# A list of steps in a new order: loads, lead-in, key rows, operand sums, x transposes and stores of an attention-and-MLP kernel

## The chip, the cores and the metric

The kernel runs on one core of a Trainium2 chip. Time is device microseconds of one execution; the number compared is the median of several runs. A core has five instruction streams that run side by side: TensorE (PE, matrix products; the loading of its weights is shown apart as PEld), VectorE (DVE), ScalarE (ACT), GpSimd (POOL) and SyncE (SP). Each works through its instructions in order and stops at one whose semaphores have not come yet. Transfers are issued by one of these streams (here POOL and SP) and carried out by 16 DMA engines.

## The reference

The inputs are q, k and v of shape 4 x 8 x 768 x 64 (batch, heads, tokens, head size), w_in 512 x 2048 and w_out 2048 x 512, all float32. Cut to what is computed:

```python
k_sum = k.reshape(B, H, 24, 32, D).max(axis=3)      # one key per block of 32 tokens
v_sum = v.reshape(B, H, 24, 32, D).mean(axis=3)
scores_l = where(|i - j| < 16, q @ k.T / 8, -1e9)    # local window
scores_s = q @ k_sum.T / 8 + log(32)                 # 24 block summaries
a = softmax(concatenate([scores_l, scores_s], -1))
x = a @ concatenate([v, v_sum])                      # then heads side by side: 3072 x 512
h = x @ w_in
out = (h * sigmoid(1.702 * h)) @ w_out               # 3072 x 512
```

## The kernel before

The work is cut by batch (768 tokens, four batches) and a batch into two halves of 384 tokens. Every step has a name, and the whole program is one list of 1001 such words, ORDER (line 35 on). The loop at the end of the kernel calls the step for each word in turn. A wrapper (line 28, the line that the profile gives for nearly every instruction) keeps the instructions of each engine in the order in which they were called. A word is a name and arguments separated by dots: numbers are the batch, half, head pair or tile and often the PSUM bank, and a last letter a, d or g puts a copy or sum on ACT, DVE or POOL. So the list sets, for each engine and each queue of transfers, what stands behind what; how far engines run apart is left to the semaphores.

The steps that the change and the prediction name:

- Loads, all issued by POOL: Lk, Lq, Lv (keys, queries, values of batch 0), Li (w_in in five pieces, two of 256 KB and three of 512 KB in float16), Lo (w_out in four), and lk, lq, lv for the later batches, one head or one strip each. Eight semaphores serve these loads, so a load waits until the eighth before it has landed. gate.1 and gate.2 are tiny POOL copies that hold the loads behind them back until a value strip or an x transpose is there.
- Lead-in of batch 0: T and Q turn keys and queries on PE, To and Qc copy them out, km takes key maxima of blocks; sm, so, sx, em, ed, ex, bt, bx make the scores and exponentials of the first half, vt and vc the block sums of v, ao, ab, ae the weighted values, vn the division by the row sum, xt and xc the transpose of x. lo, lh, lr, vo, vr, cv, ck, ow lay out keys and values for the common path; mk and mf are the masks.
- Common path: s are scores of a half and head pair, e their exponentials, m the mask, v the weighted values, nn the division, t and c (batches 0 and 1) or d (batches 2 and 3, a DMA transpose on SP) the transpose of x. Keys and queries are turned on PE for batch 1 (tk, kc, tq, qc, xm, kh, kr) and by DMA transposes on SP for batches 2 and 3 (xk, xq, then xa, ka, kR for block maxima, halos and rows). ha, sd, vm and vb make the halo and block-sum rows of the values; ha and sd are DMAs on SP.
- First product f (x by w_in, 128 columns of w_in by 384 tokens, four matmuls each, into PSUM tile ph), then g, the activation into gT.
- Second product p.t.w: the product with w_out for two strips of 128 tokens by a seven-product scheme. It reads gT, operand sums of gT (gs, the last number is the kind: product 5 reads kind 0, 6 kind 1, 7 kind 2, 3 kind 3), w_out and operand sums of w_out (ws: product 5 reads 0, 6 reads 1, 7 reads 2, 4 reads 3). x takes a product out of PSUM, o stores a strip on SP.
- P7.0 closes the pool "even", which holds the buffers of batches 0 and 2 (kx0, qT0, vw0); with the argument 0 nothing is opened in its place.

The stages follow one another, with attention of the next batch laid between the second products of this one: lead-in, first products of batch 0, its second products with scores and values of batch 1, first products of batch 1, and so on to the second products of batch 3.

```python
    for word in ORDER.split():
        name, *args = word.split(".")
        ops[name](*[engines[a] if a in engines else ...])
```

Of the kernel before, what the change touches and what calls it, by code (L numbers as in the profile page):

```python
# [45 lines left out]
lk.1.2 lv.1.5.1 lk.1.5 lk.1.6 lq.1.2 lk.1.7 m.1.1 lq.1.1 lv.1.0.0 lq.1.4 lq.1.5 lq.1.7 lv.1.3.1 lq.1.6 lv.1.0.1
lv.1.2.0 lv.1.1.0 cv.1 lv.1.1.1 lv.1.4.0 lv.1.2.1 f.0.8.k0123.2 lv.1.4.1 late m.1.3 ws.0.0 g.0.8 f.0.9.k0123.3
f.0.11.k0123.0 g.0.9 f.0.10.k0123.1 v.0.1.0.40 v.0.1.1.41 lv.1.3.0 nn.1.0 g.0.11 lv.1.5.0 g.0.10 v.0.1.2.50 v.0.1.3.51
nn.1.1 f.0.12.k0123.2 g.0.12 f.0.13.k0123.3 g.0.13 t.1.0.42 c.1.0.d f.0.14.k0123.1 g.0.14 f.0.15.k0123.0 t.1.1.52
c.1.1.d f.1.0.k01.2 f.1.8.k01.3 f.1.1.k0123.1 ws.1.0 g.0.15 g.1.1 f.1.0.k23 ws.2.0 f.1.8.k23 g.1.0 g.1.8 ws.0.1 ws.1.1  # L50
# [10 lines left out]
lv.2.1.0 lq.2.1 lv.2.0.1 lq.2.4 lv.2.3.1 lv.2.4.0 lq.2.6 m.1.0 lv.2.4.1 p.1.6 lq.2.5 p.1.2.0 x.1.6.a s.1.0.2.52
s.1.0.3.42 e.0.2 p.2.1.2 e.0.3 p.1.7 x.1.7.a s.1.1.2.52 e.1.2 s.1.1.3.42 e.1.3 x.1.2.a m.0.2 x.2.1.a p.1.3 x.1.3.a
lq.2.7 o.0.1.0.0.2 v.1.0.0.50 m.1.3 v.1.0.1.51 p.1.4 x.1.4.a o.0.1.1.0.2 p.2.5.1 x.2.5.a m.0.3 v.1.1.0.40 v.1.1.1.41
nn.0.0 p.2.6 x.2.6.a nn.1.0 t.0.0.52 m.1.2 c.0.0.a p.2.2.3 x.2.2.a t.1.0.42 c.1.0.a p.2.7 x.2.7.a v.1.0.2.50
v.1.0.3.51 nn.0.1 v.1.1.2.40 v.1.1.3.41 p.2.3 x.2.3.a o.0.2.0.0.2 p.2.4 t.0.1.52 f.0.1.k01.0 nn.1.1 x.2.4.a
o.0.2.1.0.2 f.0.8.k01.1 f.0.9.k01.3 c.0.1.d f.0.0.k01.2 G f.0.0.k23 t.1.1.42 c.1.1.d f.0.8.k23 f.0.9.k23 f.0.1.k23
g.0.0 g.0.8 g.0.1 g.0.9 xk.0.0.0 xk.0.0.1 xk.0.1.0 xk.0.1.1 xq.0.0 xq.0.1 f.1.0.k0123.2 f.1.8.k0123.1 g.1.0
f.1.1.k0123.0 g.1.8 g.1.1 f.1.9.k0123.3 g.1.9 gs.0.2.0 gs.0.2.1.g gs.0.2.3 f.0.2.k0123.2 g.0.2 f.0.10.k0123.0
f.1.2.k0123.1 xa.0.0 g.1.2 gs.0.2.2.d g.0.10 f.1.10.k0123.3 g.1.10 f.0.3.k0123.2 g.0.3 f.1.3.k0123.1 g.1.3 gs.2.2.2.d
f.1.11.k0123.3 g.1.11 ha.2.2.0 xa.1.0 gs.2.2.0 f.0.11.k0123.0 g.0.11 gs.2.2.1 gs.2.2.3 f.0.4.k0123.2 g.0.4  # L70
# [894 lines left out]
```

## Time and profile before

| | us |
|---|---|
| median of 3 runs | 211.71 |
| the runs | 211.71, 211.21, 211.89 |
| span of the profiled execution | 211.4 |
| PE busy | 198.6 (94%) |
| DVE, ACT, POOL busy | 128.1, 117.4, 109.1 |
| lead-in, to the steady first products | 26.3 |
| second products of batch 0 begin | 51.1 |
| first products of batches 1, 2, 3 begin (on both halves) | 77.3, 125.3, 168.5 |
| last matmul ends | 207.7 |

The page gives the profiled execution no time of its own beside its span; its span lies 0.3 us under the median. The profile has one row for a group of instructions: engine, operation, what it writes and reads, count and duration. A wait row has the engine, what waited, what it waited for, and total, times and longest. The chain follows the work that ended last back to the start: PE holds 71% of it, transfers 15%. The granted clock is full (1.00) in every stage up to the last.

### The profile page before, as it was taken

Reading aid. Unit: us, or ns where it says so; the run is one execution under the profiler, and the core shown is the slowest. Engines: PE = TensorE matmul, PEld = TensorE weight load, DVE = VectorE, ACT = ScalarE, POOL = GpSimd, SP = SyncE. Lnnn points to the kernel's source line nnn. Section 1 sums busy time; section 2 is a strip of 40 time slices with the busy share of each in tenths; the row PEclk is TensorE's granted clock in tenths of the full one; section 3 lists DMA queues with packets and bytes.
Section 4 is the critical chain, followed back from the end, with each engine's and each line's share of the span. In section 5 each row is a group of like instructions: output and inputs, shape, how many; then the busy total and the mean of one; then the engine's idle time right before and its main releaser. Section 6 shows DMA issues by size and latency. Waiting matters only on the chain.

```text
span 211.4 us, 5837 instructions
## 1 busy us (share of the span) xinstructions
PE 198.6 (94%) x2416; PEld 143.2 (68%) x2416; DVE 128.1 (61%) x311; ACT 117.4 (56%) x227; POOL 109.1 (52%) x157
## 2 busy tenths in 40 slices
...
GB/s 73 159 166 192 206 224 212 179 136 123 98 155 191 161 166 180 132 149 126 151 159 202 166 161 169 196 169 87 3 99 68 188 99 0 0 3 0 99 102 99
DMA packets 96458, 27.74 MB, mean 131 GB/s; under 512 B 85024, under 2 KB 93488, under 8 KB 96432
## 3 DMA queue, kind: packets, MB, share of 16 engines
...
HBM read 27.26 MB, written 6.29 MB: 159 GB/s over the span
## 4 chain that ended last, share of the span: by engine, by line
PE 71%; DMA 15%; POOL 9%; issue 2%; DVE 2%; POOLq 0%
PE ph L28 31%; PE poA L28 19%; PE poB L28 9%; DMA w_out_sb<-in_moe_w_out_dram 7%; DMA kb<-in_k_dram 4%; PE poC L28 4%; DMA xT<-x 4%; PE ps_s L28 3%; PE ps_av L28 2%; POOL v0n L28 2%; POOL w_in_sb L28 2%; POOL kx L28 2%; PE ps_t L28 1%; POOL kb L28 1%; POOL qb L28 1%
## 5 line engine op out<-in xcount | busy, mean ns | idle before, releaser
L28 PE MATMUL ph<-xT,w_in_sb 128*128 128x384 f16 x512 | 86.0, 326 | 0.7 <-DMA xT<-x 0.7
L28 ACT ACTIVATE gT<-ph 128x384 f16<-128x384 f32 x128 | 58.7, 495 | 23.8 <-PE ph L28 22.9
L28 PEld LDWEIGHTS <-w_in_sb 128*128 128x128 f16 x512 | 49.2, 98 | 32.3 <-issue 0.9
L28 PEld LDWEIGHTS <-gs 128*128 128x128 f16 x384 | 36.3, 98 | 4.7
L28 PEld LDWEIGHTS <-gT 128*128 128x128 f16 x288 | 27.5, 98 | 3.7
L28 DVE TENSOR_TENSOR gs<-gT 128x768 f16<-128x768 f16 (+1 forms) x36 | 17.1, 490 | 21.1 <-ACT gT L28 21.0
L28 ACT ACTIVATE a_sb<-ps_s 128x768 bf16<-128x768 f32 x32 | 24.5, 808 | 9.0 <-PE ps_s L28 8.9
...
L28 PE MATMUL poA<-ws,gs 128*128 128x256 f16 x192 | 24.9, 273 | 0.0
L28 POOL TENSOR_TENSOR gs<-gT 128x768 f16<-128x768 f16 x4 | 6.9, 1727 | 33.9 <-ACT gT L28 33.9
L28 ACT ACTIVATE s<-poA 128x256 f32<-128x256 f32 x14 | 5.4, 384 | 20.3 <-PE poA L28 19.0
L28 DVE TENSOR_TENSOR a_sb<-a_sb,mk 128x768 bf16<-128x768 bf16 x28 | 14.6, 549 | 3.0 <-POOL mk L28 1.9
L28 DVE TENSOR_TENSOR x<-ps_av,rc 128x768 f16<-128x768 f32 (+1 forms) x18 | 15.6, 868 | 0.6
L28 POOL TENSOR_TENSOR gs<-gs,gT 128x768 f16<-128x768 f16 (+1 forms) x6 | 8.4, 1404 | 13.0 <-DVE gs L28 12.9
L28 DVE TENSOR_TENSOR gs<-gT,gs 128x768 f16<-128x768 f16 (+1 forms) x19 | 9.2, 489 | 6.1 <-POOL gs L28 5.5
L28 PE MATMUL poB<-ws,gs 128*128 128x256 f16 x96 | 12.5, 273 | 0.0
L28 PE MATMUL poB<-w_out_sb,gs 128*128 128x256 f16 x96 | 12.5, 273 | 0.0
L28 PE MATMUL poA<-ws,gT 128*128 128x256 f16 x96 | 12.5, 273 | 0.0
L28 PE MATMUL poC<-w_out_sb,gT 128*128 128x256 f16 x96 | 12.4, 273 | 0.0
L28 PE MATMUL poA<-w_out_sb,gT 128*128 128x256 f16 x96 | 12.3, 273 | 0.0
...
## 6 DMA issues: line engine op xcount, KB each, us to landing
out_dram<-osb SPq DMA_DIRECT2D x23, 256.0 KB, 3.5
kb<-in_k_dram POOLq DMA_DIRECT2D x24, 96.0 KB, 6.0
qb<-in_q_dram POOLq DMA_DIRECT2D x24, 96.0 KB, 5.5
...
kb<-in_k_dram POOLq DMA_DIRECT2D x4, 192.0 KB, 4.2
```

The lines of the kernel that those rows point to most:

```text
L28: r = f(*a, **kw)
```

## The change

Only ORDER changes: the same 1001 steps stand in another order, with other PSUM banks, and some copies and sums on another engine. In words:

- Loads of batch 0: the first query load goes ahead of the keys, all of batch 0 ahead of w_in; the loads of batch 1 begin ahead of the last piece of w_in, and three of the four quarters of w_out are strewn among them (Lo.1, then Lo.3, Lo.0 and Lo.2; Lo.2 is the 38th load). The value loads of batch 2 and gate.1 move.
- Lead-in: the edges of the values (cv), vo and the rows of keys come earlier, vr near the end; all scores of batch 0 come ahead of the first f. To, Qc, vc, xc and lo change engines.
- Operand sums: five of the eight ws move behind the first second product of batch 0; gs are dealt anew, with 20 on POOL in the list instead of 11.
- Key rows: kR.0 and ka.0 of batch 2 come before vb and the sums of gT, ka.0 on DVE; kh and kr of batch 1 change engines.
- x transposes: d.1.1 and d.1.0 of batch 2 change places. P7.0 moves from the end of the list into the first products of batch 2. In the built program, xk.1.0.1 and xk.1.0.0 (batch 3) stand ahead of d.1.1 and d.1.0 in SP's queue, although the list has them behind.
- Stores and the copies x move within the second products; the last ones stay last.

The diff, cut to the parts spoken of:

```diff
 ORDER = """
-start Lk.0 X Lk.1 id Lq.0.0 Lk.2 Lk.3 Lq.0.1 Lv.0 Lv.1 Lv.2 cs I.10.512 sel on T.0.2 Li.1 Lv.3 To.0.a ba I.2.128 km.0
-sm.0.42 Li.0 sm.1.52 T.1.1 To.1.a Lq.1.0 Lq.1.1 I.3.128 Q.0.0.0 Qc.0.0.a Qc.0.1.d so.0 sx.0 km.1 T.2.1 To.2.a so.1
-sx.1 T.3.0 em.2 ed.0 ex.0.1 ex.0.0 bt.0.1 bx.0 To.3.d Q.0.1.0 Qc.0.2.d sm.2.42 so.2 sx.2 Qc.0.3.d sm.3.52 Li.4 so.3
-sx.3 km.2 vt.0.2.1 vc.0.2.d km.3 ao.0.40 ao.1.41 ab.0 ab.1 ae.1 ae.0 vn.0 vn.1 ed.1 ex.1.0 bt.1.0 ex.1.1 lh.3.g bx.1
-vt.2.1.1 vc.2.1.d ao.2.2 xt.0.3 lh.0.d ab.2 xc.0.d lh.1.g ae.2 vn.2 vt.3.1.1 vc.3.1.a ao.3.1 ck.0 xt.1.3 lo.0.g lh.2.g
-xc.1.a ab.3 lo.1.g ae.3 vn.3 cvs vr Li.2 lr.0.g lr.1.g Q.1.0.42 Qc.1.0.a Qc.1.1.a s.0.1.0.52 e.1.0 Li.3 Lo.0 vo.0.d
-xt.2.0 xt.3.1 vo.1.d mk.0 Lo.2 mk.1 Lo.1 Lo.3 xc.2.a xc.3.a f.0.0.k01.2 Q.1.1.0 Qc.1.2.a s.0.1.1.42 e.1.1 ow.0 cv.0
-sd.0.0.3 ha.0.2.3 sd.0.1.3 ha.0.3.3 ha.0.0.3 lk.1.0 f.0.0.k23 ha.0.1.3 Qc.1.3.d s.0.1.2.52 f.0.1.k01.3 e.1.2
+Lq.0.0 cvs Lk.0 start id on I.10.512 Lk.1 Lk.2 ba I.2.128 Q.0.0.1 ow.1 T.0.2 I.3.128 T.1.0 cs To.0.d Lq.0.1 Qc.0.1.a X
+Lk.3 Qc.0.0.a Lv.1 ck.0 To.1.a sm.0.42 Lv.0 T.2.0 Lv.2 sm.2.52 sel Q.0.1.1 mk.0 so.0 To.2.d Lv.3 Lq.1.0 em.0 km.0
+Qc.0.2.a T.3.2 ow.0 sx.0 Lq.1.1 To.3.d Li.2 so.2 km.1 sm.1.42 lh.3.g ed.0 Qc.0.3.a km.2 km.3 sx.2 cv.1 so.1 sm.3.52
+cv.0 vt.0.2.1 ex.0.1 sx.1 so.3 ex.0.0 vc.0.2.a ed.1 bt.0.2 lr.0.g bx.0 ex.1.0 ao.0.40 vt.2.1.2 sx.3 ex.1.1 ao.1.41
+ab.1 lo.1.g lo.0.d ab.0 bt.1.3 ao.2.1 vo.1.d ae.0 lh.0.d vc.2.1.a ae.1 lr.1.g lh.1.g Q.1.0.52 vt.3.1.0 Li.0 bx.1
+ao.3.2 vn.0 Qc.1.0.a lh.2.g Qc.1.1.a s.0.1.0.52 vo.0.d e.1.0 ab.2 Li.1 vn.1 ae.2 Q.1.1.3 vc.3.1.a vn.2 Li.3 s.0.1.1.42
+ab.3 ha.0.2.3 Qc.1.3.d Qc.1.2.a e.1.1 ae.3 mk.1 xt.1.0 xt.2.1 xt.0.3 s.0.1.3.42 xc.1.a xc.2.a vn.3 xc.0.d s.0.1.2.52
+e.1.3 xt.3.2 vr e.1.2 mf sd.0.1.3 xc.3.d m.1.2 ha.0.3.3 f.0.0.k01.0 f.0.1.k01.1 sd.0.0.3 f.0.0.k23 f.0.4.k0123.40
+ha.0.0.3 g.0.0 lv.1.2.1 f.0.6.k0123.50 ha.0.1.3 lv.1.1.0 f.0.5.k0123.41 f.0.1.k23 f.0.7.k0123.51 g.0.6 g.0.4 ck.1
+f.0.8.k0123.0 Li.4 Lo.1 g.0.1 g.0.8 f.0.10.k0123.2 late g.0.7 m.1.3 f.0.9.k0123.1 f.0.11.k0123.0 lk.1.0 g.0.5 lv.1.5.0
...
-f.1.3.k0123.2 g.1.3 f.1.11.k0123.1 g.1.11 gs.2.2.0 gs.2.2.1 gs.2.2.2 f.1.12.k0123.3 gs.2.2.3 g.1.12 f.1.4.k0123.2
-tk.0.52 kc.0.a f.1.13.k0123.0 g.1.13 ws.3.1 g.1.4 f.1.5.k0123.1 g.1.5 tk.1.52 gs.4.2.2 kc.1.a f.1.14.k0123.3 tk.2.42
-kc.2.a f.1.6.k0123.2 g.1.6 gs.4.2.0 gs.4.2.1 gs.4.2.3 gs.6.1.2 g.1.14 gs.6.1.0 gs.6.1.1 gs.6.1.3 f.1.7.k0123.1 g.1.7
-f.1.15.k0123.0 g.1.15 gs.7.1.0 tk.3.52 tq.0.42 kc.3.d gs.7.1.1 gs.7.1.2 p.0.1.2 x.0.1.a kh.1.1.d xm.0.1 kr.0.1.d
-ha.1.3.0 kh.0.1.d p.1.1.3 qc.0.a p.0.5.1 x.0.5.a ha.1.2.0 tq.1.52 qc.1.a p.0.6 x.0.6.a tq.2.42 gs.7.1.3 qc.2.a xm.1.1
+g.0.12 Lo.3 c.1.1.d lv.1.3.1 lv.1.5.1 f.1.6.k0123.3 f.1.3.k0123.1 g.1.6 f.1.14.k0123.2 g.1.14 lk.1.2 f.1.2.k0123.0
+g.1.3 tk.0.52 ws.0.1 f.1.0.k01.2 f.1.9.k0123.1 g.1.2 lq.1.1 kc.0.a f.1.0.k23 lk.1.5 lk.1.3 gs.6.1.0 xm.0.1
+f.1.11.k0123.0 g.1.9 kr.0.1.d f.1.7.k0123.3 G f.1.15.k0123.1 Lo.0 g.1.11 g.1.0 f.1.1.k0123.0 lv.1.0.0 g.1.7 lk.1.6
+ws.2.1 g.1.15 g.1.1 gs.6.1.1 lv.1.2.0 lk.1.7 f.0.15.k0123.2 ws.1.1 gs.7.1.0 f.1.12.k0123.1 gs.6.1.2 gs.7.1.2
+f.1.8.k01.0 f.1.8.k23 tk.2.52 g.1.12 Lo.2 g.1.8 kc.2.a lq.1.4 lq.1.5 lq.1.2 gs.0.2.2 tq.0.42 lq.1.7 f.1.10.k0123.3
+f.1.4.k0123.1 g.1.10 tk.1.52 kh.0.1.d gs.2.2.2 gs.0.2.0 g.1.4 qc.0.d gs.7.1.1 f.1.13.k0123.3 g.0.15 f.1.5.k0123.0
+xm.2.1 p.0.1.2 g.1.5 gs.2.2.0 s.1.0.0.42 g.1.13 kc.1.d gs.0.2.1 lq.1.6 ws.0.0 gs.4.2.0 p.1.1.3 p.0.5.1 e.0.0 x.0.1.a
+tk.3.52 lq.1.3 gs.4.2.1 lv.1.4.1 x.0.5.a kc.3.a gs.2.2.1 gs.6.1.3 p.0.2.0 ws.1.0 lv.1.1.1 p.0.6 ws.2.0 lv.1.0.1
+x.0.2.a lv.1.3.0 lv.1.4.0 x.0.6.a gs.4.2.3 gs.0.2.3 gs.4.2.2 gs.2.2.3 gs.7.1.3.g tq.2.52 qc.2.a xm.1.1 x.1.1.a p.1.2.0
+p.0.7 ha.1.3.0 kr.1.1.d p.0.3 tq.3.42 lk.2.4 tq.1.52 kh.1.1.g x.0.3.a p.1.6 ha.1.2.0 qc.3.d xm.3.1 kr.2.1.d kh.2.1.g
+vm.1.42 vb kr.3.1.g x.0.7.a qc.1.a s.1.0.1.52 kh.3.1.g p.1.5.1 lq.2.4 x.1.6.a e.0.1 ws.3.0 s.1.1.0.52 x.1.5.a lq.2.0
+lq.2.1 s.1.1.1.42 p.1.7 lv.2.0.1 ws.3.1 e.1.1 p.0.4 e.1.0 lk.2.0 lk.2.5 lq.2.3 s.1.0.3.42 s.1.0.2.52 p.1.3 e.0.3
...
-s.1.1.1.52 e.1.1 m.0.1 vm.1.42 vb sd.1.1.0 kr.2.1.g kh.3.1.d sd.1.0.0 xm.3.1 kr.3.1.d p.1.5.1 gate.1 lv.2.3.0 lv.2.1.1
+f.0.3.k0123.1 f.1.2.k0123.0 g.1.9 gate.1 lq.2.6 f.1.0.k0123.3 g.1.2 g.0.3 f.1.11.k0123.2 f.1.13.k0123.1 xk.0.0.0 g.1.0
...
-f.1.4.k0123.1 g.1.4 f.1.12.k0123.3 g.1.12 f.0.12.k0123.0 f.0.5.k0123.2 g.0.12 ka.0.g f.1.5.k0123.1 g.0.5
-f.0.13.k0123.0 g.0.13 f.1.13.k0123.3 g.1.5 f.0.6.k0123.2 vm.2.42 g.1.13 g.0.6 gs.4.2.0 gs.4.2.2.d vb sd.2.0.0
-f.1.6.k0123.1 sd.2.1.0 f.0.14.k0123.0 g.1.6 g.0.14 f.1.14.k0123.3 gs.4.2.1 g.1.14 gs.6.1.0 f.1.7.k0123.2 ha.2.0.0
-g.1.7 f.0.15.k0123.0 ha.2.3.0 g.0.15 gs.6.1.1 f.0.7.k0123.1 g.0.7 kR.0.d f.1.15.k0123.3 g.1.15 gs.7.1.0 X gs.6.1.3
-p.0.1.2 s.2.0.1.52 e.0.1 s.2.0.0.42 lv.3.1.0 lk.3.0 lk.3.4 lv.3.1.1 lk.3.2 gs.7.1.1 lk.3.7 lk.3.3 ha.2.1.0 x.0.1.d
+f.0.15.k0123.1 f.1.5.k0123.2 g.0.15 gs.2.2.2.d xq.0.1 lv.2.4.1 xa.1.0 lk.3.0 vm.2.42 f.0.13.k0123.1 g.1.5
+f.1.15.k0123.2 kR.0.d g.1.10 lv.3.4.1 f.0.7.k0123.0 g.0.13 f.1.14.k0123.3 f.0.4.k0123.1 vb g.0.7 g.1.14 f.0.5.k0123.0
+ka.0.d g.1.15 gs.2.2.0 lv.3.3.1 g.0.4 f.1.7.k0123.3 s.2.0.0.52 lv.3.1.0 g.0.5 s.2.0.1.42 o.0.2.0.0.2 gs.0.2.1.g
+gs.6.1.0 gs.0.2.3 gs.4.2.2.d p.0.1.0 g.1.7 p.0.2.2 e.0.0 gs.4.2.0 p.1.1.3 gs.7.1.0 gs.2.2.1.g sd.2.0.0 sd.2.1.0
+x.0.1.d gs.7.1.1 gs.7.1.2.g o.0.2.1.0.2 lk.3.4 gs.4.2.1 gs.6.1.1.g o.0.1.1.0.2 gs.7.1.3 x.0.2.a m.0.0 e.0.1 gs.2.2.3
...
-x.1.3.a o.1.1.0.0.2 nn.0.1 d.0.1 p.2.1.2 x.2.1.d p.1.4 v.2.1.0.40 v.2.1.1.41 nn.1.0 x.1.4.d v.2.1.2.50 v.2.1.3.51
-nn.1.1 p.2.5.1 x.2.5.a d.1.0 p.2.6 d.1.1 gate.2 lq.3.6 p.2.2.3 x.2.6.a p.2.7 x.2.7.a p.2.3 G x.2.2.a x.2.3.a
-o.1.2.0.0.2 p.2.4 x.2.4.a f.0.1.k01.0 f.0.9.k01.3 f.0.0.k01.2 f.0.0.k23 xk.1.1.0 xk.1.0.1 f.0.8.k01.1 f.0.8.k23
-p.2.4 x.2.4.d P7.0 o.3.1.1.0.2 o.3.2.1.0.1
+x.1.5.a p.1.3 lk.3.7 p.2.5.1 v.2.1.2.50 X lk.3.3 x.1.7.a o.1.0.1.0.2 d.0.0 d.0.1 v.2.1.0.40 lv.3.0.0 x.2.5.a
+v.2.1.1.41 x.1.3.a G v.2.1.3.51 nn.1.1 p.2.1.2 lq.3.1 x.2.1.d lk.3.2 o.1.1.0.0.2 p.1.4 d.1.1 p.2.2.0 nn.1.0 lv.3.2.1
+x.1.4.a lv.3.5.1 p.2.6 p.2.3 x.2.2.a x.2.6.a gate.2 lv.3.3.0 p.2.7 x.2.3.a d.1.0 x.2.7.a f.0.0.k01.1 f.0.9.k01.3 P7.0
+f.0.1.k01.0 xk.1.0.1 f.0.9.k23 lk.3.5 f.0.0.k23 lv.3.4.0 f.0.1.k23 g.0.9 g.0.0 xk.1.0.0 p.2.4 xk.1.1.1 g.0.1
+f.0.4.k0123.1 x.2.4.d f.1.2.k0123.0 g.1.2 f.1.10.k0123.2 f.1.1.k0123.3 lv.3.0.1 g.0.4 f.0.8.k01.0 g.1.10 g.1.1
+"""
```

More of the change, by code (lines that the diff above doesn't have):

```diff
@@ L46 @@
[L46 to L50, printed above, removed]
@@ L61 @@
[L61 to L65, printed above, removed]
@@ L66 @@
[L66 to L70, printed above, removed]
@@ new lines @@
+v.1.1.1.41 lk.2.1 o.0.0.1.0.2 lv.2.0.0 x.2.6.a x.1.7.a x.2.5.a nn.0.0 nn.1.0 p.2.7 p.2.2.0 p.1.4 m.1.2 t.1.0.52
+o.0.1.0.0.2 t.0.0.42 c.1.0.d lk.2.6 p.2.3 c.0.0.a v.1.0.2.50 x.2.7.a lk.2.3 x.2.2.a v.1.0.3.51 lv.2.1.1 x.2.3.a
+v.1.1.2.40 v.1.1.3.41 lk.2.2 lq.2.2 f.0.8.k01.1 p.2.4 nn.0.1 lv.3.1.1 t.0.1.52 x.2.4.d f.0.1.k01.0 x.1.4.a lq.2.5
+c.0.1.d f.0.9.k01.3 f.0.0.k01.2 f.0.9.k23 nn.1.1 f.0.0.k23 f.0.1.k23 f.0.8.k23 G t.1.1.42 xk.0.0.1 g.0.0
+f.0.11.k0123.2 g.0.9 g.0.8 g.0.11 c.1.1.d g.0.1 f.1.8.k0123.1 f.1.1.k0123.3 lv.2.5.0 lq.2.7 g.1.8 g.1.1 f.1.9.k0123.2
@@ new lines @@
+f.0.3.k0123.1 f.1.2.k0123.0 g.1.9 gate.1 lq.2.6 f.1.0.k0123.3 g.1.2 g.0.3 f.1.11.k0123.2 f.1.13.k0123.1 xk.0.0.0 g.1.0
+lv.2.3.0 xa.0.0 g.1.13 xk.0.1.1 f.0.2.k0123.0 lv.2.2.1 lv.2.4.0 g.1.11 f.0.6.k0123.3 f.1.3.k0123.1 g.0.2 xk.0.1.0
+g.0.6 lv.2.5.1 f.0.12.k0123.2 f.0.10.k0123.0 lv.2.2.0 g.1.3 gs.0.2.0 g.0.12 f.1.4.k0123.3 xq.0.0 gs.0.2.2.g
+f.1.6.k0123.2 lv.2.3.1 g.1.4 g.0.10 f.1.12.k0123.1 g.1.12 f.1.10.k0123.0 g.1.6 lv.2.1.0 f.0.14.k0123.3 g.0.14
+f.0.15.k0123.1 f.1.5.k0123.2 g.0.15 gs.2.2.2.d xq.0.1 lv.2.4.1 xa.1.0 lk.3.0 vm.2.42 f.0.13.k0123.1 g.1.5
```

71 lines of the change are left out of this document (34 added, 37 removed).

## The prediction

> **What bounds the kernel now.** I read the page's busy shares and its chain first, then the waits of TensorE (PE), then the stages, and inside a stage the timelines of the engines that PE waits for. The page:
>
> ```profile
> PE 198.6 (94%) x2416; PEld 143.2 (68%) x2416; DVE 128.1 (61%) x311; ACT 117.4 (56%) x227; POOL 109.1 (52%) x157
> PE 71%; DMA 15%; POOL 9%; issue 2%; DVE 2%; POOLq 0%
> ```
>
> PE is the bound: 94% busy of a span of 211.4 us. After the change the list holds the same matmuls, so only PE's idle time and its thin first stage can move. Its idle time by what ended it (total, times, longest):
>
> ```profile
> PE ps_s L28 <- issue: 1.8, 1, 1.8
> PE ps_t L28 <- DMA kb<-in_k_dram: 1.0, 1, 1.0
> PE ph L28 <- DMA xT<-x: 0.7, 1, 0.7
> PE ps_av L28 <- DMA vw<-vw: 0.7, 1, 0.7
> PE ps_s L28 <- DVE kx L28: 0.3, 1, 0.3
> ```
>
> And by stage (start:end, length, then the busy time of PE, PEld, DVE, ACT and POOL, the granted clock, DMA share, GB/s):
>
> ```profile
> 0.00:26.30 26.30, 21.71 (x390) 13.11 (x390) 18.64 (x67) 14.12 (x26) 24.37 (x47) 1.00 1.39 159
> 26.30:51.10 24.80, 23.11 (x218) 14.86 (x211) 18.25 (x39) 18.09 (x38) 16.28 (x27) 1.00 1.68 179
> 51.10:77.30 26.20, 25.91 (x446) 21.73 (x445) 21.65 (x55) 14.84 (x25) 20.93 (x32) 1.00 1.51 149
> 99.60:125.30 25.70, 23.20 (x361) 19.28 (x360) 18.04 (x44) 11.49 (x19) 14.61 (x20) 1.00 2.11 162
> ```
>
> None of these waits lies behind 125.3. So there is something to win before it (some 4 us of waits, and the lead-in up to 26.3), and behind it only something to lose. The clock is 1.00 and drops out. The first wait also shows how to count:
>
> ```profile
> 32.60 0.22 PE L28 MATMUL ps_av<-vw,a_sb 128*64 128x65 bf16 x1
> 33.50 0.67 PE L28 MATMUL ps_av<-vw,a_sb 128*64 128x65 bf16 x31 [0.68 <-DMA vw<-vw]
> ```
>
> From start to start it is 0.90, because a matmul lasts 0.22 but would let the next start almost at once. So each wait costs 0.2 more than its idle row: 0.9, 1.2 (ps_t), 2.0 (ps_s) and 0.9 (ph).
>
> **1. Lead-in.** Before, the steady run of first products begins at 26.32:
>
> ```profile
> 26.32 1.96 PE L28 MATMUL ph<-xT,w_in_sb 128*128 128x384 f16 x11
> qb<-in_q_dram POOLq DMA_DIRECT2D x2, 192.0 KB, 8.8
> w_in_sb<-in_moe_w_in_dram POOLq DMA_DIRECT2D x2, 256.0 KB, 8.1
> 8.00:12.00 4.00, 3.06 (x84) 2.07 (x78) 2.42 (x4) 3.57 (x8) 4.00 (x6) 1.00 1.83 165
> 10.06 0.53 PE L28 MATMUL ps_k<-wide,kb 128*64 128x128 bf16 x12
> L28 DVE TENSOR_REDUCE ks<-qT 128x24 bf16<-128x768 bf16 x4 | 3.8, 946 | 0.9 <-ACT qT L28 0.9
> L28 DVE TENSOR_TENSOR x<-ps_av,rc 128x384 f16<-128x384 f32 x4 | 2.2, 558 | 0.1
> L28 DVE COPY vw<-v0n 64x1536 bf16<-64x1536 bf16 x1 | 0.7, 696 | 0.0
> L28 DVE MEMSET vw<- 32x264 uint32 x4 | 1.1, 278 | 0.4
> L28 DVE COPY vs<-vs 24x128 bf16<-24x128 bf16 x4 | 0.8, 203 | 0.1
> L28 DVE COPY qT<-ps_q 128x384 bf16<-128x384 bf16 x4 | 2.1, 556 | 1.4 <-ACT qT L28 0.8 <-PE ps_q L28 0.6
> ```
>
> By the first row a first-product matmul costs (1.96 - 0.33)/10 = 0.163 us, 0.33 being the last one's own length. Ten are done ahead of 26.32, so the run could as well have begun at 24.7. The last two query loads go out near 12 and land 8.8 later, at 21; the new list takes two 256 KB pieces of w_in from ahead of them, at 165 GB/s 3.2 us, so queries come at 18. The bound is then DVE. The last key load is sixth instead of fifth, so its transposes move from 10.06 to about 11.0 and end at 11.5. Behind them DVE has To.3 0.96, three key maxima 2.84, the edges of the values (cv, moved here from later) 1.40, vo.0 and vo.1 1.39, four normalisations of 0.75 (the 558 row and a reciprocal of 0.19), lo.0 and lh.0 0.9, one Qc 0.56, vr 0.81, two copies of x transposed 0.72. That is 12.6 us: the run starts at 24.1 with four matmuls done, as if at 23.4, so 1.3 earlier. Ends: 0 (DVE idles between them as before, 7.7 of 26.3 us) and -2.3 (queries were the limit). DVE is not quite without gaps, as vn waits for PE each time; I take **-1.0**. The moves of To, Qc and vc between ACT and DVE are in this sum. Masks and constants cost nothing, since POOL makes them before the first mask at 28; one late would cost its 0.3.
>
> **2. First values.** v.0.1 needs the halo and block-sum copies, which SP issues:
>
> ```profile
> 26.48 2.36 SPq L28 DMA_DIRECT2D vw<-vw  x3
> vw<-vw SPq DMA_DIRECT2D x1, 33.0 KB, 5.1
> ```
>
> In the new list vr is next to last on DVE, done at 23.7; SP's copies behind it come 0.6 apart (2.36 for three, with gaps), the last issued at 26.3 and landed 5.1 later, 31.4. PE has 40 matmuls to do first: 23.4 + 6.5 = 30.0. So 1.4 instead of 0.9: **+0.5** (0 to +1.5).
>
> **3. Batch-1 keys and w_out.** Loads on POOL land in order of issue. Those of batch 1 now stand ahead of three quarters of w_out:
>
> ```profile
> 21.09 14.38 DMA w_out_sb<-in_moe_w_out_dram
> 35.76 9.50 DMA kb<-in_k_dram
> ```
>
> This chain, POOL waiting on w_out and tk.0 on keys issued behind it, goes. The first key pair is in with 5.4 MB, by the stages' 159 and 179 GB/s (0.6 MB of SP's counted in) at 36.3; tk.0 comes at 38.9. **-1.2**, at worst 0. The price: w_out's third quarter is now the 38th load. It is in with 8.0 MB and 0.7 of SP's, at 51.5; the operand sum that feeds the second products wants it at 52. That is cover of 0.5 us only; I take **+0.3** (0 to 2.5).
>
> **4. DVE under batch 0's second products.** Of the eight operand sums of w_out (ws, 0.69 each) five move behind the first product: ws.0.0 ahead of gs.4.2.0, which p.0.5 reads, ws.3.1 behind vb. DVE has 21.65 of 26.20 in this stage already. Step by step against the products' 0.87, p.0.5 is 0.3 late, p.0.7 0.5, p.0.4 0.8, while the 0.3 on kx goes with 0.2 behind it: **+1.1** (0 if DVE comes 1.5 early, +3 if every ws counts).
>
> **5. Scores of batch 2.** Before:
>
> ```profile
> 101.33 0.52 DVE L28 COPY kx<-ka 128x576 bf16<-128x576 bf16 x2
> 101.73 0.67 PE ps_s L28 x24
> ```
>
> kR.0 (101.33) sits behind vb and the sums of gT, and the scores behind it: 2.0. The new list puts it ahead of both, and ka.0 on DVE instead of POOL: **-2.0** (at worst 0).
>
> **6. x transposes of batch 2, on SP.** The list itself is harmless here: d.1.1 and d.1.0 stand ahead of xk.1.0.1 and xk.1.0.0. But P7.0, which closes the pool holding kx0, qT0 and vw0, moves from the end into this batch's first products, and the built program's SP queue has those two transposes of batch-3 keys *ahead* of d.1.1 and d.1.0. They wait for the last of four key loads, lk.3.2, and all behind them on SP waits too.
>
> ```profile
> 114.76 1.25 SPq L28 DMA_TRANSPOSE xT<-x  x1
> 117.39 5.70 SPq L28 DMA_TRANSPOSE xT<-x  x3
> 125.67 2.66 SPq L28 DMA_TRANSPOSE kx<-kb  x2
> 123.47 1.14 PE L28 MATMUL ph<-xT,w_in_sb 128*128 128x384 f16 x6
> DMA to landing us min/median/max: 2.8/3.9/7.9
> kb<-in_k_dram POOLq DMA_DIRECT2D x24, 96.0 KB, 6.0
> ```
>
> (The fifth row is xT's.) The products of batch 1 start at 98.3 on the new clock. POOL has three operand sums there until 101.3, then eleven issues of about 0.8 before lk.3.2, at 111; it lands at 117.0. Two xk 2.66: 119.7; d.1.1 1.25: 120.9; d.1.0 lands between 3.9 and 7.9 after that, and I take the middle, 5.9, as loads still run: 126.8. PE began these first products at 123.47; in the new list one product (0.87) moves behind that start, and the first matmul on half 1 has it and 16 first-product matmuls ahead, so 126.1 on the old clock. Parts 1 to 5 and 7's vm make that 2.0 earlier, 124.1, and with the wait for d.0, which stays behind nn.0 and is again about 0.9, it is 125.0. So 1.8 more wait on d.1.0, and with 0.3 for its own start behind two SP stores: **+2.1**. Ends: 0 (lk.3.2 issued by 109) and +5 (7.9, and two us of POOL delay).
>
> [...]
>
> **7. Small ones.** vm.2 waits for lv.2.4.1, issued behind gate.1 and a POOL sum: **+0.3** (0 to 1.4). In batch 3, gate.2 reads the late d.1.1 and holds lk.3.5, behind it xk.1.1, ka.1 and xq.1:
>
> ```profile
> POOL gate L28 <- DMA xT<-x: 8.4, 1, 8.4
> 178.81 1.51 DVE L28 TENSOR_TENSOR gs<-gT 128x768 f16<-128x768 f16 x1 [3.88 <-ACT gT L28]
> 178.27 1.63 POOL L28 TENSOR_TENSOR gs<-gT 128x768 f16<-128x768 f16 x1 [0.25 <-ACT gT L28]
> L28 DVE TENSOR_TENSOR gs<-gT,gs 128x768 f16<-128x768 f16 x12 | 6.6, 556 | 6.0 <-POOL gs L28 5.5
> ```
>
> Before, POOL waited 8.4 there and PE not at all; s.3.0 may now be **+0.5** late (0 to 2.5). POOL's operand sums rise from 11 to 20, and a DVE sum beside one took 1.51 instead of 0.556: **+0.35** (0 to 2). PE changes its kind of matmul 77 times instead of 87, at about 0.1 where it counts: **-0.2**. Copies of products (x), stores and PSUM banks: nothing, as ACT is busy 56% and DVE 61%; without that cover a copy costs its 0.4. The end, a copy and a 128 KB store, stays.
>
> [...]
>
> **Sum.** -1.0 + 0.5 - 1.2 + 0.3 + 1.1 - 2.0 + 2.1 + 0.3 + 0.5 + 0.35 - 0.2 = +0.75, say 0.8. Against the profiled execution that is a span of 212.2. The page gives it no other time; the median of the three runs is 0.3 above its span, so 212.5.
>
> **Rivals.**
> B, faster: SP's order costs nothing and batch 3 is in time. It decides by lk.3.2: issued by 109, d.1.0 is there by 125. For it speaks that POOL issued loads 0.8 apart in the old trace, against it that it waited for sums and landings too. Then 2.1 and 0.5 go: 209.9.
> C, slower: w_out's third quarter. From 52 on each us late holds DVE's queue at ws.1.0 and PE with it; the queue landed w_out 14.4 after issue at worst. 2.5 late gives 2.2 more than my 0.3: 214.7.
> D, slower: POOL's sums meet DVE's. At 0.95 for eight of the nine new ones on PE's path the 0.35 becomes 2.9, if DVE has no slack before the reader: 215.
> E, gains and losses cancel, 211.7, with lead-in at -1.8.
>
> **Chances.** Forecast 212.5, 38%, its own range 212.4 to 214.2; B 30%, C 13%, D 7%, E 12%. The range 209.3 to 215.6 reaches from B with more of the lead-in to the ends of C and D. A measurement here tells some 0.3% from no change: faster 0.30, same 0.12, slower 0.58.
>
> **What will show it.** The steady run of first products from about 24; v.0.1 waiting on vw<-vw 1.4; no wait of ps_t on kb, none of ps_s near 100; ph waiting on xT some 2.5 in sum; on SP kx<-kb ahead of the last two xT<-x. I am wrong if poA or poB waits for w_out or ws, if xT's wait is below 1, or if DVE idles in the lead-in as before.

## The result, and the profile after

The changed kernel takes 220.12 us (median of 4 runs, 217.27 to 220.28); the kernel before took 211.8 beside it (4 runs, 211.21 to 214.69). The ratio is 1.0352, with a 95% interval of 1.0272 to 1.0432. The prediction was 212.5, with a range up to 215.6: the sign was right, the size was not. The profiled execution took 220.11 with a span of 218.4; in the runs that have both, the time is some 1.7 us above the span, so the profiled execution of the kernel before, with its span of 211.4, took about 213.1, above its median. Spans are compared with spans below: 218.4 against 211.4, 7.0 more. The medians lie 8.3 apart, so about 1.3 of the difference is not in this pair of profiles.

First the busy line of the page and PE's waits in the changed kernel (total, times, longest):

```profile
PE 200.5 (92%) x2416; PEld 143.8 (66%) x2416; DVE 138.2 (63%) x299; ACT 112.4 (51%) x225; POOL 122.6 (56%) x171
PE ps_av L28 <- DMA vw<-vs: 2.8, 1, 2.8
...
PE poA L28 <- DVE s L28: 1.7, 3, 1.0
PE ps_s L28 <- DMA qT<-qb: 1.5, 1, 1.5
...
PE ps_av L28 <- DMA vw<-vw: 0.9, 1, 0.9
PE poB L28 <- DVE osb L28: 0.9, 1, 0.9
PE ph L28 <- DMA xT<-x: 0.6, 1, 0.6
```

The waits that the change was forecast to remove are gone: none of ps_t on kb, and none of ps_s near 100. Three others have come: the first values on the copies of value rows (vw), products on DVE (poA, poB), and the scores of batch 3 on their queries. Two numbers of the first line matter for later. PE is busy 2 us longer with the same 2416 matmuls, and DVE 10 us longer (138.2, before 128.1) although it has fewer instructions (299, before 311).

The largest loss is at the first values. The timeline of PE there, and the same stretch by windows (start:end, length, busy time of PE, PEld, DVE, ACT and POOL with their counts; the third number from the end is the granted clock):

```profile
25.11 6.87 PE L28 MATMUL ph<-xT,w_in_sb 128*128 128x384 f16 x40
...
34.78 0.19 PE L28 MATMUL ps_av<-vw,a_sb 128*64 128x65 bf16 x1 [2.80 <-DMA vw<-vs]
35.89 1.28 PE L28 MATMUL ps_av<-vw,a_sb 128*64 128x65 bf16 x47 [0.92 <-DMA vw<-vw]
37.10 3.99 PE L28 MATMUL ph<-xT,w_in_sb 128*128 128x384 f16 x16
```

```profile
26.00:33.00 7.00, 5.94 (x36) 3.25 (x34) 2.23 (x8) 5.76 (x12) 5.91 (x8) 1.00 1.26 167
33.00:36.00 3.00, 0.30 (x8) 0.25 (x10) 0.00 (x0) 0.27 (x1) 0.70 (x1) 1.00 1.42 205
36.00:38.00 2.00, 2.00 (x50) 1.47 (x49) 1.38 (x4) 0.00 (x0) 0.68 (x1) 0.55 2.34 155
38.00:40.00 2.00, 2.00 (x9) 0.99 (x8) 0.91 (x1) 0.66 (x2) 1.82 (x3) 0.60 1.58 189
40.00:42.00 2.00, 2.00 (x22) 1.48 (x21) 0.53 (x2) 1.19 (x3) 2.00 (x3) 1.00 1.75 181
```

The run of 40 first products ends near 32. The first value matmul starts at 34.78, the second at 35.89: 4.1 us lost from start to start, against 0.9 before. Behind this gap the granted clock is 0.55 and 0.60 for four microseconds. Sixteen matmuls take 3.99 there, where the pace of the kernel before makes 15 x 0.163 + 0.33 = 2.8, and the 47 value matmuls 1.28 instead of about 0.93 (48 take 0.95 with the halos first, below); that is 1.6 more. The one run of the four at 217.27 had a mean clock of 0.998, the others 0.984 to 0.992, as if the clock had fallen in those three; the mean does not say where. In this profile, then, 3.9 us almost without a matmul are followed by 0.55 to 0.60 of the clock for about 4 us; going by the mean clocks, that was not so in every run. Less idle time came ahead of a low clock too: the profile of the run with exchanged key loads, below, has 0.50 behind a wait of only 1.0.

Where the 7.0 us came from, start to start, with the terms of the prediction:

| place | before | after | difference | predicted |
|---|---|---|---|---|
| lead-in, first products as if begun at | 24.7 | 25.1 | +0.4 | -1.0 |
| first values: gap, then half clock | 0.9 | 4.1 + 1.6 | +4.8 | +0.5 |
| tk on keys | 1.2 | 0 | -1.2 | -1.2 |
| w_out; DVE in batch 0's products | 0.5 | 0.9 | +0.4 | +0.3, +1.1 |
| batch 2 scores and the products around | 2.0 | 1.5 | -0.5 | -2.0 |
| x transposes of batch 2 | 0.9 | 0.8 | -0.1 | +2.1 |
| batch 3: scores, then products on DVE | 0 | 3.2 | +3.2 | +0.85 |
| last products, on DVE | 0 | 0.6 | +0.6 | 0 |

With the forecast's -0.2 for PE's own order, which no row here measures, that is +7.4, within 0.4 of the 7.0 found. The lead-in row holds for this pair of executions alone (see part 1, below).

### The profile page after: what moved, and what is told of

It reads as the page before. It is cut to its first block, busy times and chain, and to the rows that moved or that the text cites. A ratio compares the mean times of both kernels' runs of the same rounds, so it can differ in the third digit from the quotient of the medians.

```text
span 218.4 us, 5834 instructions
## 1 busy us (share of the span) xinstructions
PE 200.5 (92%) x2416; PEld 143.8 (66%) x2416; DVE 138.2 (63%) x299; ACT 112.4 (51%) x225; POOL 122.6 (56%) x171
## 5 line engine op out<-in xcount | busy, mean ns | idle before, releaser
L28 PE MATMUL ph<-xT,w_in_sb 128*128 128x384 f16 x512 | 87.4, 329 | 0.7 <-DMA xT<-x 0.6
L28 ACT ACTIVATE gT<-ph 128x384 f16<-128x384 f32 x128 | 57.0, 491 | 42.1 <-PE ph L28 41.0
L28 PEld LDWEIGHTS <-w_in_sb 128*128 128x128 f16 x512 | 49.7, 99 | 33.3 <-issue 1.6
L28 DVE TENSOR_TENSOR gs<-gT 128x768 f16<-128x768 f16 (+1 forms) x31 | 20.3, 678 | 23.0 <-ACT gT L28 22.8
L28 POOL TENSOR_TENSOR gs<-gT 128x768 f16<-128x768 f16 (+1 forms) x9 | 14.3, 1595 | 34.0 <-ACT gT L28 34.0
L28 PEld LDWEIGHTS <-gT 128*128 128x128 f16 x288 | 27.8, 98 | 4.0
L28 POOL DMA_DIRECT2D qb<-in_q_dram x28 | 23.3, 844 | 1.6 <-POOLq L949 0.8
L28 DVE TENSOR_TENSOR a_sb<-a_sb,mk 128x768 bf16<-128x768 bf16 x28 | 16.5, 614 | 2.3 <-ACT a_sb L28 2.3
L28 PE MATMUL poB<-w_out_sb,gs 128*128 128x256 f16 x96 | 12.6, 273 | 0.1
L28 POOL TENSOR_TENSOR gs<-gs,gT 128x384 f16<-128x384 f16 (+1 forms) x7 | 9.3, 1322 | 5.8 <-DVE gs L28 5.8
L28 DVE TENSOR_REDUCE ka<-kx 128x48 bf16<-128x1536 bf16 x4 | 7.0, 1747 | 6.8 <-DMA kx<-kb 6.8
```

What stands on the lines that cost most here:

```text
L28: r = f(*a, **kw)
```

## The experiments

Ratios are to the kernel before, run beside each, with 95% intervals. The runs of one kernel scatter by 2 to 4 us, in part with the lead-in (the profiles have the first products from 24.1 to 25.1 in the new order), so an interval is about 0.7% to either side, and readings rest on traces as much as on times.

**The x transposes (part 6).** P7.0 goes back to the end, which restores SP's order.

```diff
-f.0.9.k01.3 P7.0 f.0.1.k01.0 ... x.2.4.d o.3.2.1.0.1
+f.0.9.k01.3 f.0.1.k01.0 ... x.2.4.d P7.0 o.3.2.1.0.1
```

> The changed kernel with P7.0 back at the end of the list, so that SP issues the last two x transposes of batch 2 ahead of the two key transposes of batch 3. The prediction's part 6 says that this order costs 2.1 us: then 218.0. What the changed trace shows (the wait of ph on xT is 0.6 idle, as before the change) says it costs little: 219.5 to 220.3.

Measured: 219.14, ratio 1.0313 (1.0241 to 1.0386), not to be told from the changed kernel. SP in the changed kernel, then in this one:

```profile
119.46 3.11 SPq L28 DMA_TRANSPOSE xT<-x  x2
...
123.38 2.70 SPq L28 DMA_TRANSPOSE kx<-kb  x2
126.19 2.70 SPq L28 DMA_TRANSPOSE xT<-x  x2
```

```profile
119.73 3.11 SPq L28 DMA_TRANSPOSE xT<-x  x2
122.94 0.54 SPq L28 DMA_DIRECT2D out_dram<-osb  x1
123.58 2.60 SPq L28 DMA_TRANSPOSE xT<-x  x2
```

```profile
PE poB L28 <- DVE osb L28: 1.9, 1, 1.9
...
PE ps_s L28 <- DMA qT<-qb: 0.4, 1, 0.4
```

The key transposes did stand ahead, and did delay the others by 2.6, yet PE waited 0.6 for it: lk.3.2 had landed by 120.2, before SP was through with d.0 and a store, d.1.0 landed 2.7 after its issue instead of 5.9, and PE itself came 5 us later than I had put it. In this kernel the waits on xT and on the queries are gone or smaller (0.6 to none, 1.5 to 0.4), and the wait of poB on DVE has grown from 0.9 to 1.9. The late transfers stood in front of a late DVE, and most of what is saved on them is waited for there.

**The clock by itself.** 28 matmuls that nobody reads keep PE busy in the gap.

```diff
-lk.1.1 lk.1.4 v.0.1.2.40
+lk.1.1 lk.1.4 J.28 v.0.1.2.40
```

> The changed kernel with 28 matmuls without use (128 x 224, into a free PSUM bank) put ahead of the first values of batch 0, so that TensorE is busy while it waits for the halo rows there. It adds work and takes no wait away. Theory G, that the long idle stretch there lowers the granted clock behind it (0.55 to 0.60 from 36 to 40 us) and that this costs about 2 us of its own: 217.5 to 218.5, granted clock 1.00 from 36 to 40, and the mode near 217 becomes the rule. Rival, that the clock is a side show hidden by other waits: 220 or somewhat more.

```profile
36.00:38.00 2.00, 2.00 (x14) 1.22 (x13) 1.66 (x3) 0.98 (x2) 1.35 (x2) 1.00 2.18 164
38.00:40.00 2.00, 2.00 (x22) 1.45 (x20) 1.24 (x3) 1.13 (x3) 2.00 (x4) 1.00 1.36 197
```

Measured: 218.85, ratio 1.0304 (1.0227 to 1.038). The clock is 1.00 where the values come as late as before, so it was PE's idleness that lowered it. By the ratios the time is 0.5% (1.0 us) lower than the changed kernel's, but the intervals overlap, so the size rests on the traces: from the second value matmul to the run of 20 first products it is 5.7 in the changed kernel (35.89 to 41.60) and 4.1 here (34.76 to 38.89), the 1.6 read above.

**The gap: filled, or mended.** One kernel puts the first values 12 matmuls later, with the two halves of the heads exchanged; the other gives SP the four halo copies, which need only vo, ahead of the two sum copies, which need vr.

```diff
-lk.1.4 v.0.1.2.40 g.0.10 v.0.1.3.41 v.0.1.0.50 v.0.1.1.51 f.0.2.k0123.0 lq.1.0 nn.1.1 f.0.3.k0123.2 nn.1.0 f.0.13.k0123.1 f.0.14.k0123.3 ...
+lk.1.4 g.0.10 f.0.2.k0123.0 lq.1.0 f.0.3.k0123.2 f.0.13.k0123.1 g.0.2 g.0.3 g.0.13 v.0.1.0.40 v.0.1.1.41 v.0.1.2.50 v.0.1.3.51 nn.1.0 f.0.14.k0123.3 ...
```

> The changed kernel with the first values of batch 0 put three first products (12 matmuls, 2.0 us) later, and the first half of the heads ahead of the second. If the gap there is a fixed landing time of SP's copies, the moved matmuls fill it: the gap falls from 3.7 idle to about 1.8 and the clock stays at 1.00: 216 to 217. If the copies are late because PE's own pace sets them (a wait that moves along), nothing is gained: 219.5 to 220.3.

```diff
-ab.3 ha.0.2.3 Qc.1.3.d ... sd.0.1.3 xc.3.d m.1.2 ha.0.3.3 ... sd.0.0.3 ... ha.0.0.3 ... ha.0.1.3
+ab.3 ha.0.2.3 ha.0.3.3 ha.0.0.3 ha.0.1.3 Qc.1.3.d ... sd.0.1.3 xc.3.d m.1.2 ... sd.0.0.3
```

> The changed kernel with one edit on SP's queue: the four halo copies of batch 0, which need only the copies of v (done near 22 us), go ahead of the two block-sum copies, which need vr (done at 25.4). Theory H, that the halos are late because they stand behind the sums on SP and the last copies land at 35.8 for that reason: they go out from 22, the last of all lands at 31 to 32, PE's gap of 4.1 falls under 1 and the clock stays at 1.00: 215 to 216. Rival, that the landing is set by the loads that share the DMA engines (7 to 8 us for a copy): the last lands at 34 or later whatever the order, 218 to 220.

Measured: 217.22, ratio 1.0216 (1.0143 to 1.0289), and 215.15, ratio 1.0121 (1.0059 to 1.0182). With the values later, PE waits 0.5 at the second value matmul (34.73) and 0.6 for ACT ahead of the moved products (31.84), and the clock is 1.00 up to 42: filling the gap is worth 1.4%. SP in the changed kernel, then SP and PE with the halos first:

```profile
25.39 0.58 SPq L28 DMA_DIRECT2D vw<-vs  x1
26.01 0.60 SPq L28 DMA_DIRECT2D vw<-vw  x1
26.66 1.31 SPq L28 DMA_DIRECT2D vw<-vs  x1
28.01 2.26 SPq L28 DMA_DIRECT2D vw<-vw  x2
```

```profile
19.06 3.15 SPq L28 DMA_DIRECT2D vw<-vw  x4
24.62 1.23 SPq L28 DMA_DIRECT2D vw<-vs  x2
```

```profile
25.81 5.41 PE L28 MATMUL ph<-xT,w_in_sb 128*128 128x384 f16 x31
31.14 0.95 PE L28 MATMUL ps_av<-vw,a_sb 128*64 128x65 bf16 x48
32.03 2.29 PE L28 MATMUL ph<-xT,w_in_sb 128*128 128x384 f16 x13
```

The halo copies could all go at 19 to 22, but only the first did (19.8); three stood behind the sums, and those behind vr. Here all six land by 30.5, 4.4 to 6.7 after issue. With the order changed PE goes through the values without a gap and the clock stays at 1.00. One queue's order cost 2.3% here, two thirds of the whole loss. The rival (a landing set by the shared DMA engines, whatever the order) is refuted as the cause of the gap.

**POOL's sums.** All 20 operand sums of gT on POOL go to DVE; then the same for the 11 of the kernel before.

```diff
-gs.0.2.2.g   (and 19 more with g)
+gs.0.2.2.d   (and 19 more with d)
```

> The changed kernel with all 20 operand sums of gT that it has on POOL put on DVE. Theory D of the prediction, that POOL sums slow DVE's own instructions beside them (sums and mask products of 0.55 us last 1 to 2 us there): DVE's busy time falls by about 10 us for the instructions it had and rises by 8 for the new ones, the waits of PE for DVE in batches 1 and 3 shrink by 2 to 3 us: 217 to 218. Rival, that DVE is short of time whoever is beside it: 220 to 222, with the waits of PE for s, osb and gs longer.

Measured: 217.05, ratio 1.02 (1.0147 to 1.0254). DVE's instructions of the same kinds, in the changed kernel, then in this one (count, then busy us and mean ns):

```profile
L28 DVE TENSOR_TENSOR a_sb<-a_sb,mk 128x768 bf16<-128x768 bf16 x28 | 16.5, 614 | 2.3 <-ACT a_sb L28 2.3
L28 DVE TENSOR_TENSOR gs<-gT 128x384 f16<-128x384 f16 x14 | 9.3, 679 | 7.7 <-ACT gT L28 7.6
L28 DVE TENSOR_TENSOR gs<-gs,gT 128x768 f16<-128x768 f16 x9 | 6.9, 786 | 0.1
```

```profile
L28 DVE TENSOR_TENSOR a_sb<-a_sb,mk 128x768 bf16<-128x768 bf16 x28 | 14.7, 550 | 2.1 <-ACT a_sb L28 2.1
L28 DVE TENSOR_TENSOR gs<-gT 128x384 f16<-128x384 f16 x16 | 5.5, 354 | 6.7 <-ACT gT L28 6.5
L28 DVE TENSOR_TENSOR gs<-gs,gT 128x768 f16<-128x768 f16 x12 | 6.5, 552 | 0.1
```

DVE does 20 instructions more and is busy 130.7 instead of 138.2. The half-sized sums cost 0.679 on average beside POOL and 0.354 without. Some sums of batch 2 at the start of its second products in the changed kernel, DVE's and POOL's timelines (the first DVE line holds a full sum and a half-sized one), and the stage around by windows:

```profile
148.08 2.27 DVE L28 TENSOR_TENSOR gs<-gT 128x768 f16<-128x768 f16 x2
150.26 1.99 DVE L28 TENSOR_TENSOR gs<-gs,gT 128x768 f16<-128x768 f16 x1
```

```profile
148.12 3.72 POOL L28 TENSOR_TENSOR gs<-gT 128x768 f16<-128x768 f16 x2 [0.55 <-ACT gT L28]
```

```profile
145.00:165.00 20.00, 17.33 (x218) 13.01 (x217) 19.70 (x31) 12.16 (x21) 10.76 (x7) 1.00 0.43 65
```

While POOL's two sums last, to 151.84, DVE gets two done and the third ends 0.4 later: 4.2 us for what takes 0.55, 0.35 and 0.55 elsewhere. DVE is then the bound, 19.70 of 20.00, and PE waits for it. How long DVE's sums take beside POOL's is in these rows, by what means is not. The gap and the half clock at the first values are still in this kernel, and it has a new wait of 1.7 at its batch-2 values. Those begin at 114.8 and 115.1, as the last two halo copies land, which SP issued from 105.1 on, behind two stores.

> The kernel before with its own 11 POOL sums of gT put on DVE. Theory D2, that a POOL sum costs only where DVE has work of its own beside it that PE waits for: before, most stand in batch 3's first products where DVE idles, so nothing or little changes: ratio 0.997 to 1.003. Rival, that any POOL sum slows the kernel: ratio 0.985 to 0.995.

Measured: 212.47, ratio 0.9978 (0.9939 to 1.0017), no difference that can be told. That fits the theory that a POOL sum costs only where DVE has work that PE waits for, with few such places in the kernel before. It does not show it by itself: in this run's profile PE has new waits of 1.3 and 1.0 for DVE's sums near 148, so the move may have a price of its own.

**Batch 3's queries by themselves.** xq.1.0 ahead of the value copies on SP, lq.3.6 ahead of ka.1 on POOL.

```diff
-vb g.1.12 lq.3.3 sd.3.1.0 ... lq.3.7 g.0.3 ... gs.6.1.0 xq.1.0 g.1.13 ... lq.3.6 f.1.5.k0123.0
+vb g.1.12 lq.3.3 xq.1.0 sd.3.1.0 ... lq.3.7 lq.3.6 g.0.3 ... gs.6.1.0 g.1.13 ... f.1.5.k0123.0
```

> The changed kernel with the queries of batch 3 alone mended: xq.1.0 ahead of the value copies on SP, lq.3.6 ahead of ka.1 on POOL. The trace has PE wait 1.5 there (ps_s for qT from qb, near 150). If it is a wait of its own: 1.2 to 1.5 under the changed kernel, so 217.5 to 219. If DVE's late sums behind it swallow the gain: 219.5 to 220.3.

```profile
PE ps_av L28 <- DMA vw<-vs: 3.2, 1, 3.2
PE poB L28 <- DVE osb L28: 2.5, 1, 2.5
```

Measured: 220.3, ratio 1.0353 (1.0287 to 1.0419), so nothing. The wait on queries (1.5) is gone and the next one, of poB on DVE, went from 0.9 to 2.5. The rival held: this wait, with a later engine behind it, cost nothing.

**The gains by themselves, in the kernel before.** kR.0 ahead of vb; and lk.1.1 exchanged with lk.1.3.

```diff
-gs.4.2.2.d vb sd.2.0.0 ... g.0.7 kR.0.d f.1.15.k0123.3
+gs.4.2.2.d kR.0.d vb sd.2.0.0 ... g.0.7 f.1.15.k0123.3
```

> The kernel before with one part of the change alone: kR.0 of batch 2 ahead of vb and the last sums on DVE. By the prediction's part 5 the wait of 2.0 at 101.7 goes and nothing takes its place: 209.7. Rival: the DVE queue is late as a whole there, so what kR gains the sums behind it lose, and the next products wait for sums or for a bank that DVE frees, by 1 to 1.5 us: 210.9 to 211.7.

```profile
PE ps_s L28 <- DVE vs L28: 1.1, 1, 1.1
...
PE poA L28 <- DVE s L28: 0.7, 1, 0.7
...
PE ps_s L28 <- issue: 0.6, 1, 0.6
...
PE poB L28 <- DVE gs L28: 0.3, 1, 0.3
```

Measured: 213.03, ratio 1.0019 (0.9978 to 1.0061). The wait of 1.8 became four of 0.6, 1.1, 0.3 and 0.7: DVE was late as a whole there, as the rival said.

```diff
-g.0.3 lk.1.3 lq.1.0 ... lk.1.4 lk.1.1 lk.1.2
+g.0.3 lk.1.1 lq.1.0 ... lk.1.4 lk.1.3 lk.1.2
```

> The kernel before with two key loads of batch 1 exchanged (lk.1.1 to where lk.1.3 was), so that the first head pair is loaded earlier. By the prediction's part 3 the wait of ps_t on kb, 1.2 from start to start at 45.3, goes: 210.5. Rival: the second pair or the sums behind are then late by as much: 211.5 to 212.

Measured: 214.11, ratio 1.0061 (1.0015 to 1.0107). The wait of ps_t on kb is gone from the profile; PE waits 0.7 each for values near 69 and for sums near 149 (poB on gs) instead. That execution's steady first products began 1.5 later (27.8), with a wait of 1.0 for a key load in the lead-in and half the clock behind it. By windows:

```profile
9.00:11.00 2.00, 1.00 (x28) 0.65 (x23) 1.21 (x2) 1.80 (x3) 2.00 (x4) 0.98 1.76 164
11.00:13.00 2.00, 2.00 (x38) 0.89 (x38) 0.96 (x1) 0.58 (x2) 2.00 (x3) 0.50 2.37 154
```

No gain either way.

**Put together.** First: halos first, P7.0 at the end, queries early, and 13 of 20 sums back on DVE.

> The changed kernel with all that its trace blames undone: halos ahead of sums on SP in batch 0, 13 of the 20 operand sums back from POOL to DVE, P7.0 at the end, and xq.1.0 with its loads earlier in batch 3. If the parts add up (4.5 for the gap and the clock, 3 for the sums, 1.3 for the queries): 210.5 to 212. If they cover for one another, as waits behind a wait do: 213 to 215.

Measured: 211.92, ratio 0.9975 (0.9928 to 1.0021): the loss is gone. The parts had been put at 8.8 us together (4.5, 3 and 1.3), and about 8.0 came (1.0352 less 0.9975, of 212). In its profile PE still waits 1.3 for DVE beside POOL sums of batch 2 and 0.9 for halos of batch 2. So, next, these two places:

```diff
-gs.0.2.2.g ... gs.2.2.2.g   (batch 2; five sums stay on POOL)
+gs.0.2.2.d ... gs.2.2.2.d
-s.2.0.1.42 o.0.2.0.0.2 ... ha.2.0.0 ... ha.2.2.0 ... ha.2.3.0 ... ha.2.1.0
+s.2.0.1.42 ha.2.0.0 ha.2.2.0 ha.2.3.0 ha.2.1.0 o.0.2.0.0.2
```

> The mended kernel (halos ahead of sums on SP, P7.0 at the end, queries of batch 3 earlier, 7 sums on POOL) with two more edits: the two sums of batch 2 that ran beside DVE's go to DVE too, which leaves 5 on POOL, and the halo copies of batch 2 go ahead of its block sums and of three stores on SP. In the mended kernel's profile these two places cost 1.4 and 1.2 us. If that is what PE waits for: span 209.3 - 2.5 = 207, and 2 to 2.5 us under the kernel before measured beside it per point (ratio 0.985 to 0.99). If DVE or SP is then late elsewhere: as the mended kernel, ratio 0.995 to 1.0.

```profile
PE 198.3 (96%) x2416; PEld 143.6 (69%) x2416; DVE 131.4 (63%) x314; ACT 112.5 (54%) x225; POOL 101.8 (49%) x156
PE ph L28 <- DMA w_in_sb<-in_moe_w_in_dram: 1.0, 1, 1.0
```

Measured: 210.11, ratio 0.9874 (0.9824 to 0.9924); the profiled execution, at 208.68, has a span of 207.0. It beats both kernels: 1.3% under the one before and about 4.6% under the changed one (0.9874/1.0352). PE is 96% busy; behind 30 us its waits are all under 0.5. So there is a gain of about 2.7 us (1.6 to 3.7) in the mended list, which five choices in the new list hid. Not all of it is the new order's: the kernel before has its halo copies behind the sums too, with 0.9 lost at the first values, and halos first were not tried in it.

The last one takes four memsets (cv.1) out of the lead-in.

```diff
-sx.2 cv.1 so.1 ... sd.0.1.3 xc.3.d m.1.2
+sx.2 so.1 ... sd.0.1.3 xc.3.d cv.1 m.1.2
```

> As the one before, and the edges of the values for batch 1 (cv.1, four memsets, 0.7 us on DVE) moved from the lead-in to behind the last copy of x. If DVE bounds the lead-in, as the prediction's part 1 says, the run of first products begins 0.7 earlier and the time falls by 0.5 to 0.7 against the one before. If what bounds it is PE behind late loads: no difference, 0 to 0.2.

Measured: 210.45, ratio 0.9892 (0.9846 to 0.9938), the same as without. DVE's last copy of x came 0.45 earlier in its profile (24.26, before this edit 24.71) and the first products 0.8 earlier (23.75 instead of 24.51), as forecast, but PE then waited 1.2 for DVE (poB on osb) under batch 1's second products, where it had not; nothing came through in the time.

## Why the prediction was wrong

Two terms were far too small: the first values (part 2, +0.5 forecast and 4.8 found) and the operand sums on POOL (part 7, +0.35 forecast and about 3 by the run that takes them off POOL).

- **What bounds it, and the sign.** Right: PE, with something to win before 125.3 and something to lose behind it. Batch 3's scores and the products around them, where PE never waited before, lost 3.2. But the largest loss, 4.8, came ahead of 125.3.
- **Part 1, the lead-in (-1.0).** +0.4 in this pair of profiles, but the pair does not settle it. The count of DVE's work was right (12.6 predicted; from To.3 at 12.75 to the last copy of x at 25.68 it is 12.9, with an idle time of 0.2). What moved is when it starts: I let the last key transposes follow their load, at 11.0, but PE has the query transposes of Q.0.1 in front of them in the new list, and those wait for their own load. In the changed kernel's profile:

```profile
11.02 0.53 PE L28 MATMUL ps_q<-wide,qb 128*64 128x128 bf16 x12 [0.94 <-DMA qb<-in_q_dram]
...
12.18 0.53 PE L28 MATMUL ps_k<-wide,kb 128*64 128x128 bf16 x12
```

  That wait is 0.3 or less in the eight other profiles with this lead-in (every other variant of the new order but the last, which changes the lead-in itself): their key transposes come at 11.1 to 11.6 and their first products at 24.1 to 24.6, not 25.1. The old lead-in in turn is later in the profiles of the kernel before with kR.0 early and of the one with exchanged key loads than in the kernel before itself: counted as if begun at once, 25.5 and 26.2 instead of 24.7. The first products with halos first, then those with kR.0 early, where ten were done ahead:

```profile
24.35 6.87 PE L28 MATMUL ph<-xT,w_in_sb 128*128 128x384 f16 x40
```

```profile
27.15 6.70 PE L28 MATMUL ph<-xT,w_in_sb 128*128 128x384 f16 x38
```

  So a gain in the lead-in is likely; its size stays open.
- **Part 2, the first values (+0.5).** The step that failed most. The mechanism was right, SP's copies behind a late vr, and three sizes were off: vr was done at 25.4 instead of 23.7, SP's issues took up to 1.4 instead of 0.6, and two of the last three landed 7 to 8 us after issue where I took 5.1, the shortest of the old trace's six copies there (5.1 to 6.0). Behind the gap of 3.9 us the granted clock then fell to 0.55 and 0.60, and I had dropped the clock in the first paragraph because it had been 1.00: the gap's price went from 3.2 to 4.8. The range had +1.5 at most.
- **Part 3, keys and w_out.** tk's wait went as forecast (-1.2), and the last piece of w_out landed at 53.0, before DVE's next sum of it began at 55.2. POOL's loads did land in order of issue, all 105 of them in the profile before and in the one after. Rival C did not come about. But the exchange of keys in the kernel before shows that such a gain need not come through.
- **Part 4.** About right in kind and too large: +0.4 for +1.1.
- **Part 5 (-2.0).** The wait went and 1.5 came back on the products behind it, as DVE freed a PSUM bank late. The step that failed is that the whole 2.0 was counted, as if no later wait would take the place of this one; the run of this part alone gained nothing.
- **Part 6 (+2.1).** The order on SP was as read, the price was not: -0.1. PE, late by the earlier losses, arrived with the transposes, and d.1.0 landed in 2.7 instead of 5.9. Undoing it gave no time that can be told.
- **Part 7.** The POOL sums (+0.35) were the other large miss, and rival D, at 7%, was the right mechanism: 3 us by the run that takes them all off POOL. The row with 1.51 for 0.55 was at hand, and I counted such meetings as rare instead of counting, stage by stage, where DVE has no slack. The queries of batch 3 were late as forecast (1.5 for +0.5), but by themselves worth nothing. The 0.1 for a change of kind is in the trace before: groups of eight second-product matmuls follow one another 0.87 apart (145.78, 146.65), and the scores come 0.97 behind the second group (147.62). What ten changes fewer are worth (-0.2) no run shows.
- **The base.** Span and time differ by 1.7, not by 0.3. This did not hurt the forecast, since 0.8 on the median of 211.71 is also 212.5; but the profile from which all was read is of an execution of about 213.1.
- **The signs.** Of the three signs of being wrong two came up: poA waited 0.5 for ws, and xT's wait was 0.6. DVE did not idle in the lead-in as before.
